# A fused Fourier mixing and GEGLU kernel: the gate of three blocks a batch from two matmuls instead of three, and the channel-128 rows read one slot later

## The chip, the cores and the metric

The kernel runs on one core of a Trainium2 chip. The metric is the device time of one execution in microseconds. TensorE (PE) multiplies, VectorE (DVE), ScalarE (ACT) and GpSimd (POOL) do the elementwise work, and SyncE (SP) issues most DMAs.

## The reference

The input x is 8 batches of 3008 tokens with 256 channels, fp32. The reference takes the real part of a two-dimensional Fourier transform of each batch and puts the result, as 24064 tokens of 256 channels, through a GEGLU block:

```python
X = np.fft.fft(np.fft.fft(x, axis=1), axis=2).real
g = X @ w_gate                       # 256 x 1536
gelu = 0.5 * g * (1.0 + erf(g * inv_sqrt2))
out = (gelu * (X @ w_val)) @ w_out   # 1536 x 256
```

## The kernel before, in words

**Symmetry.** The real part of the transform of a real input repeats itself: the token with index -t and channel -c equals the token t and channel c. The kernel therefore forms only half of the tokens of a batch, in a layout with the channels on the 128 partitions, as an even part E and an odd part O (the two planes of the tile `EO_sb`). The weights are transformed the same way on the chip. The gate of a token is g(E) + g(O), and that of its mirror token is g(E) - g(O) but for one channel, number 128: its row sits in partition 0 of the odd plane although it doesn't change its sign. A third copy of the gate's odd weights, `W["g", "M"]`, is the odd weights times -2, with 0 in that channel. So a gate takes three matmuls into one PSUM bank: E, then O (now the bank holds the token's gate), then M (now it holds the mirror's). The value takes two: E, then O; VectorE makes the mirror's value as 2 (E + correction) - value, where the correction is the channel-128 row (broadcast over the partitions in `EB_sb`) times the weight column `yw`.

**Slots.** Half a batch is 1505 tokens in three chunks of 512, 512 and 481. The 1536 hidden columns are twelve blocks of 128. One (chunk, block) pair is one slot: 36 slots a batch, 288 in all. The function `feed` writes the order of every engine's queue out by hand, slot by slot (the scheduler is off). In a slot stand, in this order:

- `G`: `l1_gate` of this block, matmuls E and O into a bank of `ps_g` (two banks), and the gelu of it on ScalarE (L676)
- `g`: `l1_gate2` of the block before, matmul M and the mirror's gelu (L685)
- `V`: `l1_value` of this block, matmul E into a bank of `ps_v` (three banks), and on VectorE `ve` = EB yw + E (L704)
- four output matmuls (L749) of the chunk before into `ps_o` (one bank)
- POOL's folds of a later batch's input (L216 to L224), where `plan` puts one
- `v`: `l1_value2` of the block before, matmul O, the product h of the token on VectorE (L720), the mirror's value on VectorE (L722), and the mirror's product h on POOL (L724)
- four more output matmuls; after every sixth piece of four, an evacuation of `ps_o` on ScalarE (L769) and four output stores on SyncE's queue (L654)
- the fills, where `plan` puts one: pieces of the Fourier transform of the next batches

All gate, value and mirror matmuls go through one helper, `mm`, and have its line, L660.

**The transform's fills.** For a batch b, `s1t` multiplies folded input by the first factor and evacuates to `S_sb` (L546, L549); `z_write` and `z_read` turn the layout by way of DRAM. Then, for each chunk, `tp_y` computes the channel-128 row and writes it to DRAM (L612, L616, L618), `tp_e` and `tp_o` compute the even and the odd plane of `EO_sb` (L582, evacuated by ScalarE in L592), and `tp_rows` reads the row back twice: into all 128 partitions of `EB_sb` (L626) and into partition 0 of the odd plane of `EO_sb` (L628). The odd planes of the three chunks share a tile, and `tp_o` of a chunk waits for the EO row read of the chunk before. `load_part` loads the input of a later batch: the forward half by SyncE (L152, into `x_raw`) and the mirrored half by an indirect DMA of POOL (L158). `plan` puts these fills at slots: for batches 4 to 7 the nine pieces `tp_y`, `tp_e`, `tp_o` of three chunks lie in slots 18 to 33 of the batch before, for batches 1, 2 and 3 nearer together.

The order within SyncE's queue follows the order of the calls, so that the slot of a fill settles which stores, loads and row writes stand ahead of it.

**Buffers named below.** `gelu` has 5 buffers, `ve` 3, `v` 4, `ps_g` 2, `ps_v` 3, `ps_o` 1 and `ps_dft` (the fills' bank) 2.

Of the kernel before, what the change touches and what calls it, by code (L numbers as in the profile page):

```python
# [9 lines left out]
FP32 = mybir.dt.float32  # L10
BF16 = mybir.dt.bfloat16
AF = mybir.ActivationFunctionType
ALU = mybir.AluOpType
# [15 lines left out]
def kernel(  # L29
# [104 lines left out]
    def v_tile():  # L134
        return work([128, TOK], FP32, "v", 4, "v_sb")

    def osb_tile():
        return work([128, 2, C], FP32, "osb", 3, "out_sb")

    def psum(tag):  # L140
        bufs = {"g": 2, "v": 3, "o": 1, "dft": 2}[tag]
        return psum_pool.tile([128, 512], FP32, tag=tag, bufs=bufs, name=f"ps_{tag}")
# [100 lines left out]
    keep2 = const_pool.tile([128, 1], FP32)  # L243
    dump = const_pool.tile([1, 1], FP32)
    one_h = const_pool.tile([1, 1], BF16)
    yw = const_pool.tile([128, NFC], FP32)
    NGP = NJ * NK
    ff = work([128, 2 * NGP], FP32, "EO", 2, "ff")
    rr = work([128, 2 * NGP], FP32, "EO", 2, "rr")
# [218 lines left out]
    def make_yw(f0, n):  # L468
# [7 lines left out]
            nc.scalar.activation(yw[:, c0 : c0 + nq], ps[:, 0:nq], AF.Copy)  # L476
        return run


    EO_bufs, EB_bufs = {}, {}  # L480
    turn = [0]
# [152 lines left out]
        return tp_e(b, gi, 1, engine)  # L634


    def store(b, gi, sub, sign, osb_half, queue):
        segs = [c for c in cols[gi] if c[0] // 128 == sub]
        m = min(128, chunk_len[gi] - sub * 128)
        for i, (off, k2, w) in enumerate(segs):  # L640
            p0 = off - sub * 128
            lo, hi = (1, w - 1) if sign and k2 == 0 else (0, w)
            if sign:
                t0 = T - k2 - N2 * (hi - 1)
                p1 = m - p0 - hi
            else:
                t0 = k2 + N2 * lo
                p1 = p0 + lo
            dst = ap_replace(
                out,  # L650
                ap=[[N2 * C, hi - lo], [1, C]],
                offset=out.offset + (b * T + t0) * C,
            )
            (nc.sync if i else queue).dma_start(out=dst, in_=_sub(osb_half, [[1, C]], 0, part_start=p1, part_num=hi - lo))  # L654

    def ffn_work(b):
# [5 lines left out]
        def cols_of(ci, fc):  # L662
# [3 lines left out]
                cstate[ci] = {"h": h_tile(), "ps": {}, "pso": {}}  # L666
            return n, c0, E, O, cstate[ci], slice(fc * 128, (fc + 1) * 128)

        def l1_gate(ci, fc):
            def run():  # L670
                n, _, E, O, st, fs = cols_of(ci, fc)
                pg = psum("g")
                mm(pg, n, "g", "E", fs, E, True, False)
                mm(pg, n, "g", "O", fs, O, False, True)
                gl = gelu_tile()
                nc.scalar.activation(gl[:, 0, :n], pg[:, :n], AF.Gelu)  # L676
                st["ps"][fc] = [pg, gl]
            return run

        def l1_gate2(ci, fc):  # L680
            def run():
                n, _, _, O, st, fs = cols_of(ci, fc)
                pg, gl = st["ps"][fc][:2]
                mm(pg, n, "g", "M", fs, O, False, True, skip_group_check=True)
                nc.scalar.activation(_sub(gl, [[-1, n]], TOK + n - 1), pg[:, :n], AF.Gelu)  # L685
            return run
# [88 lines left out]
        for ci in range(NG):  # L775
            nsub = (chunk_len[ci] + 127) // 128
            parts = {k: [f(ci, fc) for fc in range(NFC)] for k, f in (
                ("G", l1_gate), ("V", l1_value), ("g", l1_gate2), ("v", l1_value2))}
            subs = [nsub - 1, *range(nsub - 1)] if last(ci) else range(nsub)
            l2s = [l2_piece(ci, s, g, f) for s in subs for g in range(2) for f in range(0, NFC, L2P)]  # L780
            chunks.append((parts, l2s))
# [91 lines left out]
        make_yw(0, 256)()  # L873
        tp_y(0, 0)()

    NS = NG * NFC

    def plan():

        fill, pool = {}, {}  # L880

        def at(table, s, f):
            table.setdefault(s, []).append(f)

        early = []
        for gi in (1, 2):
            early += [ch(0, 2 * gi), ch(0, 2 * gi + 1, "V"), tp_e(0, gi), tp_o(0, gi, "V"), tp_y(0, gi)]
        for s, f in (
                (0, make_w(0, 256, 256)), (0, make_w(1, 256, 256, engine="V")), (1, make_yw(256, 256)),
                (1, make_w(1, 512, 512, (1,))), (2, make_w(0, 512, 512, (0,), "V")), (2, make_yw(512, 512)),  # L890
                (3, make_w(0, 512, 512, (1,))), (3, make_w(1, 512, 512, (0,), "V")),
                (4, make_w(1, 1024, 512, (1,), "V")), (5, make_w(0, 1024, 512, (0,), "V")), (5, make_yw(1024, 512)),
                (6, make_w(0, 1024, 512, (1,))), (7, make_w(1, 1024, 512, (0,), "V"))):
            at(fill, s, f)
        for i, f in enumerate(early):
            at(fill, (7, 8, 9, 10, 11, 12, 13, 14, 15, 16)[i], f)

        for k, s in ((0, 8), (1, 9), (2, 9)):
            at(fill, s, lambda k=k: load_part(2, k, (load_forward,)))
        for k, s in ((0, 18), (1, 19), (2, 19)):  # L900
            at(fill, s, lambda k=k: load_part(2, k, (load_mirror,)))

        def spread(b, items, s0, s1):

            each = len(items) // NG
            for i, f in enumerate(items):
                s = s0 + i * (s1 - s0) // (len(items) - 1)
                at(fill, s, f)
                if i % each == each - 1:
                    at(fill, s + 1, tp_rows(b, i // each))  # L910

        for b in range(1, B):
            s0 = (b - 1) * NS
            ops = []
            for j0, nj in PIECES:
                ops += fold_ops(b, j0, nj, nc.gpsimd)
            per = len(ops) // 5
            first, n = {2: (s0 - 13, 29), 3: (s0 - 19, 30)}.get(b, (s0 - 22, 32))
            slot_of = [first + i * n // len(ops) for i in range(len(ops))]
            if b == 1:  # L920
                slot_of = [4, 4, 5, 5, 6, 6, 7, 7, 8, 8, 9, 13, 13, 14, 15, 15, 16, 17, 17, 18]
            for s, f in zip(slot_of, ops):
                at(pool, s, f)
            if 1 < b < B - 1:
                for k, piece in ((0, 1), (1, 3), (2, 4)):
                    at(fill, slot_of[piece * per + 1] + 1, lambda b=b, k=k: load_part(b + 1, k))
            s = s0 - 9 if b > 1 else 12
            for i, (jg, piece) in enumerate(((2, 1), (1, 2), (0, 3), (3, 4))):
                ready = slot_of[piece * per + per - 1] + 2
                for g in range(2):  # L930
                    s = max(s + 1, ready)
                    at(fill, s, s1t(b, jg, g))
                if i == 2:
                    at(fill, s + 1, z_write(b, 0, 12))
                if i == 3:
                    at(fill, s + 1, z_write(b, 12, 4))
            at(fill, s + 2, z_read(b))
            items = []
            for gi in range(NG):
                items += [tp_y(b, gi), tp_e(b, gi), tp_o(b, gi)]  # L940
            if b == 1:
                spread(b, items, s + 6, s + 18)
                continue
            assert s + 7 < s0 + NS - 10
            spread(b, items, s + 7, s0 + NS - 3)
        return fill, pool

    def feed():
        blocks, works = [], []
        for b in range(B):  # L950
            for parts, l2s in ffn_work(b):
                works.append(l2s)
                blocks += [(parts, fc) for fc in range(NFC)]
        fill, pool = plan()
        pend, before = [], None

        first = works[0]
        sooner = {8: [first[0]], 9: [first[3]], 10: [first[1]], 11: [first[4]], 13: [first[2]], 14: [first[5]]}
        works[0] = first[6:]
        for i, (parts, fc) in enumerate(blocks):  # L960
            if fc == 0 and i:
                assert not pend
                pend = list(works[i // NFC - 1])
            two = sooner.pop(i, []) if i <= NFC + 2 else [pend.pop(0) for _ in range(2) if pend]
            parts["G"][fc]()
            if i == 0:
                behind_first_gate()
            if before:
                before[0]["g"][before[1]]()
            parts["V"][fc]()  # L970
            if len(two) == 2:
                two.pop(0)()
            for f in pool.pop(i, []):
                f()
            if before:
                before[0]["v"][before[1]]()
            if two:
                two.pop(0)()
            for f in fill.pop(i, []):
                f()  # L980
            before = parts, fc
        assert not fill and not pool
        before[0]["g"][before[1]]()
        before[0]["v"][before[1]]()
        for u in works[-1]:
            u()
# [33 lines left out]
```

## Time and profile before

| what | value |
|---|---|
| median of 3 runs | 630.27 us (629.33 to 630.61) |
| the profiled execution's own time | 629.18 us |
| its span, first to last instruction | 627.0 us |
| granted TensorE clock, mean | 0.996 |
| busy PE / DVE / POOL / ACT | 98% / 92% / 81% / 68% |
| gate and value matmuls | 1440, 0.204 or 0.217 us from start to start |

"Busy" is the share of the span in which an engine has an instruction at work. Matmuls overlap in the records, so their durations (0.37 us at 481 or 512 columns) are longer than the distance between their starts. A wait is written "engine tile line <- who ended it: us in total, times, longest". The timeline gives the start, the duration, the engine, the line, the operation and, in brackets, the idle time before it and what ended it. SPq is SyncE's queue: its rows are the issue of a DMA, not the transfer.

### The profile page before, as it was taken

Reading aid. Unit: us, or ns where it says so; the run is one execution under the profiler, and the core shown is the slowest. Engines: PE = TensorE matmul, PEld = TensorE weight load, DVE = VectorE, ACT = ScalarE, POOL = GpSimd, SP = SyncE. Lnnn points to the kernel's source line nnn. Section 1 sums busy time; section 2 is a strip of 40 time slices with the busy share of each in tenths; the row PEclk is TensorE's granted clock in tenths of the full one; section 3 lists DMA queues with packets and bytes.
Section 4 is the critical chain, followed back from the end, with each engine's and each line's share of the span. In section 5 each row is a group of like instructions: output and inputs, shape, how many; then the busy total and the mean of one; then the engine's idle time right before and its main releaser. Section 6 shows DMA issues by size and latency. Waiting matters only on the chain.

```text
span 627.0 us, 12895 instructions
## 1 busy us (share of the span) xinstructions
PE 612.3 (98%) x4195; PEld 405.1 (65%) x4243; DVE 578.3 (92%) x941; ACT 428.4 (68%) x842; POOL 505.3 (81%) x510
## 2 busy tenths in 40 slices
PE   7999999999999999999999999999999999999997
PEld 3456666666666666666666666666666666666666
DVE  8689989999899999999999998999999999999992
ACT  6777677666776677667676677676676666666661
POOL 8399999989897998879997899969988655555651
PEclk8999999999999999999999999999999999999999
DMA  9961754536353353731645335633212322221123
GB/s 177 227 97 31 210 129 116 144 105 159 99 146 101 98 133 79 184 113 46 160 110 135 101 78 127 148 97 98 62 49 63 91 86 55 51 52 39 42 51 81
DMA packets 54217, 65.40 MB, mean 104 GB/s; under 512 B 7831, under 2 KB 49802, under 8 KB 51754
## 3 DMA queue, kind: packets, MB, share of 16 engines
q1 hardware_dynamic: 47222, 49.03, 30.6%
q0 software_dynamic: 6608, 15.29, 11.4%
q8 instruction: 33, 0.54, 0.4%
q10 hardware_dynamic: 320, 0.26, 0.2%
q14 instruction: 34, 0.28, 0.2%
HBM read 39.65 MB, written 30.17 MB: 111 GB/s over the span
## 4 chain that ended last, share of the span: by engine, by line
PE 93%; ACT 2%; issue 1%; DVE 1%; DMA 1%; POOL 1%; POOLq 0%; ACTq 0%
PE ps_o L749 38%; PE ps_g L660 28%; PE ps_v L660 19%; PE ps_dft L546 2%; PE ps_dft L582 2%; PE ps_o L820 1%; DMA Z_sb<-z 1%; PE ps_dft L443 1%; PE ps_dft L612 0%; ACT gelu_sb L676 0%; POOL h_sb L724 0%; POOL eo_sb L224 0%; DMA out_dram<-out_sb 0%; ACT gelu_sb L685 0%; PE ps_dft L749 0%
## 5 line engine op out<-in xcount | busy, mean ns | idle before, releaser
L724 POOL TENSOR_TENSOR h_sb<-gelu_sb,v_sb 128x512 bf16<-128x512 bf16 (+1 forms) x280 | 319.8, 1146 | 93.1 <-DVE v_sb L722 85.9
L749 PE MATMUL ps_o<-Wo_sb,h_sb 128*128 128x256 bf16 (+1 forms) x2232 | 334.9, 273 | 0.9 <-POOL h_sb L724 0.9
L749 PEld LDWEIGHTS <-h_sb 128*128 128x128 bf16 (+1 forms) x2304 | 228.7, 100 | 112.9 <-POOL h_sb L724 2.6
L676 ACT ACTIVATE gelu_sb<-ps_g 128x512 bf16<-128x512 f32 (+1 forms) x288 | 169.4, 588 | 98.6 <-PE ps_g L660 80.9
L660 PE MATMUL ps_g<-EO_sb,W_sb 128*128 128x512 bf16 (+1 forms) x817 | 228.5, 375 | 3.8 <-ACT gelu_sb L685 0.8
L704 DVE SCALAR_TENSOR_TENSOR ve_sb<-EB_sb,yw,ps_v 128x512 f32<-128x512 bf16 (+1 forms) x280 | 206.3, 737 | 25.9 <-PE ps_v L660 25.0
L660 PE MATMUL ps_v<-EO_sb,W_sb 128*128 128x512 bf16 (+1 forms) x575 | 213.7, 375 | 0.7 <-DVE W_sb L451 0.6
L720 DVE TENSOR_TENSOR h_sb<-gelu_sb,ps_v 128x512 bf16<-128x512 bf16 (+1 forms) x280 | 189.9, 678 | 1.1 <-ACT gelu_sb L685 0.7
L660 PEld LDWEIGHTS <-W_sb 128*128 128x128 bf16 x1440 | 137.2, 98 | 81.1 <-issue 1.8
L722 DVE SCALAR_TENSOR_TENSOR v_sb<-ve_sb,ps_v 128x512 f32<-128x512 f32 (+1 forms) x280 | 187.5, 670 | 0.0
L685 ACT ACTIVATE gelu_sb<-ps_g 128x512 bf16<-128x512 f32 (+1 forms) x288 | 168.7, 586 | 0.0
L769 ACT ACTIVATE out_sb<-ps_o 128x512 f32<-128x512 f32 x92 | 55.0, 598 | 35.7 <-PE ps_o L749 35.6
L224 POOL TENSOR_TENSOR eo_sb<-ab_sb 94x512 bf16<-94x512 f32 (+1 forms) x70 | 77.6, 1111 | 0.5
L549 ACT ACTIVATE S_sb<-ps_dft 96x512 bf16<-96x512 f32 x56 | 32.9, 588 | 14.0 <-PE ps_dft L546 13.9
L592 ACT ACTIVATE EO_sb<-ps_dft 128x512 bf16<-128x512 f32 (+1 forms) x44 | 26.0, 590 | 23.3 <-PE ps_dft L582 22.1
L217 POOL TENSOR_TENSOR ab_sb<-x_raw,x_raw 94x508 f32<-94x508 f32 (+1 forms) x30 | 33.0, 1100 | 0.0
L220 POOL TENSOR_TENSOR ab_sb<-x_raw,x_raw 94x508 f32<-94x508 f32 (+1 forms) x30 | 32.9, 1098 | 0.0
L546 PE MATMUL ps_dft<-eo_sb,G 94*96 94x256 bf16 x119 | 22.5, 274 | 0.2 <-POOL eo_sb L224 0.2
L158 POOL DMA_INDIRECT x_raw<-in_x_dram,idx x18 | 17.1, 948 | 2.9 <-issue 1.1
L582 PE MATMUL ps_dft<-TP,Z_sb 128*128 128x128 bf16 (+1 forms) x184 | 17.8, 218 | 0.0
L582 PEld LDWEIGHTS <-Z_sb 128*128 128x128 bf16 x192 | 14.6, 98 | 1.8 <-DVE Z_sb L534 0.6
L546 PEld LDWEIGHTS <-G 94*96 94x96 bf16 x119 | 13.0, 123 | 1.2 <-issue 0.4
(148 smaller groups left out, 166.2 us busy)
## 6 DMA issues: line engine op xcount, KB each, us to landing
out_dram<-out_sb SPq DMA_DIRECT2D x364, 64.0 KB
x_raw<-in_x_dram SPq DMA_DIRECT2D x10, 768.0 KB
Z_sb<-z SPq DMA_DIRECT2D x7, 768.0 KB
z<-S_sb SPq DMA_DIRECT2D x7, 576.0 KB
EB_sb<-yrow SPq DMA_DIRECT2D x14, 128.0 KB
z<-S_sb SPq DMA_DIRECT2D x7, 192.0 KB
x_raw<-in_x_dram SPq DMA_DIRECT2D x2, 640.0 KB
EB_sb<-yrow SPq DMA_DIRECT2D x7, 120.2 KB
```

The source lines that it names most:

```text
L224: eng.tensor_tensor(_sub(eo, [[C, nj], [1, 128]], j0 * C + g * 128), ab(0, 0, [[1, 128]]), ab(1, 0, [[1, 128]]), op=op)
L546: nc.tensor.matmul(ps[:96, q * C : (q + 1) * C], G[:, j, :], _sub(eo, [[1, C]], j * C), start=(j == js[0]), stop=(j == js[-1]))
L582: nc.tensor.matmul(ps[:, o : o + n], st["Z"][:, pair, g * 128 : g * 128 + 128], _sub(TP, [[1, n]], g * 128), start=True, stop=True)
L660: nc.tensor.matmul(ps[:, :n], W[nm, part][:, fs], src, start=start, stop=stop, **kw)
L676: nc.scalar.activation(gl[:, 0, :n], pg[:, :n], AF.Gelu)
L685: nc.scalar.activation(_sub(gl, [[-1, n]], TOK + n - 1), pg[:, :n], AF.Gelu)
L704: nc.vector.scalar_tensor_tensor(ve[:, :n], EB_bufs[b][:, c0 : c0 + n], yw[:, fc : fc + 1], pv[:, :n], op0=ALU.mult, op1=ALU.add)
L720: nc.vector.tensor_tensor(st["h"][:, fc, 0, :n], gl[:, 0, :n], pv[:, :n], op=ALU.mult)
L722: nc.vector.scalar_tensor_tensor(_sub(vv, [[-1, n]], n - 1), ve[:, :n], 2.0, pv[:, :n], op0=ALU.mult, op1=ALU.subtract)
L724: nc.gpsimd.tensor_tensor(st["h"][:, fc, 1, :n], gl[:, 1, :n], vv[:, :n], op=ALU.mult)
L749: nc.tensor.matmul(pso[:m, half], st["h"][:, fc, sign, h0 : h0 + m], Wo_sb[:, fc, :], start=(fc == 0 and not (first and sign)), stop=(fc = ...
L769: nc.scalar.activation(_sub(osb, [[1, 2 * C]], 0, part_num=m), pso[:m, :], AF.Copy)
```

## The change

In slots 4, 28 and 33 of the batches 1 to 6 (18 blocks in all) the gate takes two matmuls. E goes into the bank alone, and ScalarE copies 2E from it to a new fp32 tile, `e2_sb` (one buffer). A new part `O`, called in `feed` behind the first four output matmuls and ahead of POOL's folds, adds O to the bank, takes the token's gelu on ScalarE, lets VectorE form EB ywg - bank into a buffer of the tag `v`, and lets POOL add `e2_sb` to it: that is the mirror's gate. In the next slot `l1_gate2` takes its gelu from there, and the matmul M is not issued. The column `ywg` is made once, in slot 14 of batch 0. Apart from that, `tp_rows` is called one slot later for every chunk and batch.

```diff
+    def e2_tile():
+        return work([128, TOK], FP32, "e2", 1, "e2_sb")
...
+    def make_ywg():
+
+        fcs = sorted({i % NFC for i in GATE2})
+        ps = psum("dft")
+        for fc in fcs:
+            nc.tensor.matmul(
+                ps[:, fc : fc + 1], W["g", "O"][0:1, fc * 128 : (fc + 1) * 128], one_h, start=True, stop=True)
+        for fc in fcs:
+            nc.scalar.activation(ywg[:, fc : fc + 1], ps[:, fc : fc + 1], AF.Copy, scale=2.0)
...
+    GATE2 = (4, 28, 33)
...
+        def two_gate(ci, fc):
+            return 0 < b < B - 1 and ci * NFC + fc in GATE2
+
         def l1_gate(ci, fc):
             def run():
                 n, _, E, O, st, fs = cols_of(ci, fc)
                 pg = psum("g")
+                if two_gate(ci, fc):
+                    mm(pg, n, "g", "E", fs, E, True, True)
+                    e2 = e2_tile()
+                    nc.scalar.activation(e2[:, :n], pg[:, :n], AF.Copy, scale=2.0)
+                    st["ps"][fc] = [pg, gelu_tile(), e2]
+                    return
                 mm(pg, n, "g", "E", fs, E, True, False)
                 mm(pg, n, "g", "O", fs, O, False, True)
...
+        def l1_gate_odd(ci, fc):
+            def run():
+                if not two_gate(ci, fc):
+                    return
+                n, c0, _, O, st, fs = cols_of(ci, fc)
+                pg, gl, e2 = st["ps"][fc][:3]
+                del st["ps"][fc][2]
+                mm(pg, n, "g", "O", fs, O, False, True, skip_group_check=True)
+                nc.scalar.activation(gl[:, 0, :n], pg[:, :n], AF.Gelu)
+                d = v_tile()
+                nc.vector.scalar_tensor_tensor(
+                    d[:, :n], EB_bufs[b][:, c0 : c0 + n], ywg[:, fc : fc + 1], pg[:, :n],
+                    op0=ALU.mult, op1=ALU.subtract)
+                nc.gpsimd.tensor_tensor(d[:, :n], e2[:, :n], d[:, :n], op=ALU.add)
+                st["ps"][fc][0] = d
+            return run
+
         def l1_gate2(ci, fc):
             def run():
                 n, _, _, O, st, fs = cols_of(ci, fc)
                 pg, gl = st["ps"][fc][:2]
+                if two_gate(ci, fc):
+                    nc.scalar.activation(_sub(gl, [[-1, n]], TOK + n - 1), pg[:, :n], AF.Gelu)
+                    return
                 mm(pg, n, "g", "M", fs, O, False, True, skip_group_check=True)
...
+        at(fill, 14, make_ywg)
...
                 if i % each == each - 1:
-                    at(fill, s + 1, tp_rows(b, i // each))
+                    at(fill, s + 2, tp_rows(b, i // each))
...
             if len(two) == 2:
                 two.pop(0)()
+            parts["O"][fc]()
             for f in pool.pop(i, []):
                 f()
```

More of the change, by code (lines that the diff above doesn't have):

```diff
@@ L245 @@
     one_h = const_pool.tile([1, 1], BF16)
-    yw = const_pool.tile([128, NFC], FP32)
+    yw, ywg = (const_pool.tile([128, NFC], FP32, name=f"yw_{i}") for i in "vg")
     NGP = NJ * NK
@@ L634, in tp_o @@
         return tp_e(b, gi, 1, engine)
+    NS = NG * NFC
+    GATE2 = (4, 28, 33)
     def store(b, gi, sub, sign, osb_half, queue):
@@ L777, in ffn_work @@
             parts = {k: [f(ci, fc) for fc in range(NFC)] for k, f in (
-                ("G", l1_gate), ("V", l1_value), ("g", l1_gate2), ("v", l1_value2))}
+                ("G", l1_gate), ("O", l1_gate_odd), ("V", l1_value), ("g", l1_gate2), ("v", l1_value2))}
             subs = [nsub - 1, *range(nsub - 1)] if last(ci) else range(nsub)
@@ L874, in behind_first_gate @@
         tp_y(0, 0)()
-    NS = NG * NFC
     def plan():
```

## The prediction

> **What bounds the kernel now.** I read the page first (busy shares, chain), then the waits by engine, then the timeline slot by slot. A slot is one block of 128 hidden columns for one chunk; a batch has 36, and "slot 4.28" is batch 4's slot 28. The page:
>
> ```profile
> PE 612.3 (98%) x4195; PEld 405.1 (65%) x4243; DVE 578.3 (92%) x941; ACT 428.4 (68%) x842; POOL 505.3 (81%) x510
> PE 93%; ACT 2%; issue 1%; DVE 1%; DMA 1%; POOL 1%; POOLq 0%; ACTq 0%
> ```
>
> TensorE carries 93% of the chain. A busy matmul row is no proof, so I take the distance between starts. TensorE in slot 4.28:
>
> ```profile
> 378.05 0.78 PE L660 MATMUL ps_g<-EO_sb,W_sb 128*128 128x481 bf16 x3
> 378.66 0.37 PE L660 MATMUL ps_v<-EO_sb,W_sb 128*128 128x481 bf16 x1
> 378.86 0.60 PE L749 MATMUL ps_o<-Wo_sb,h_sb 128*128 128x256 bf16 x4
> 379.30 0.37 PE L660 MATMUL ps_v<-EO_sb,W_sb 128*128 128x481 bf16 x1
> ```
>
> Three gate matmuls in 0.61 us: 0.204 us each at 481 columns (0.217 at 512), and nothing idle. A bare slot of 512 columns takes 1.957 us. So a matmul removed is worth 0.2 us, if nobody makes TensorE wait. Who is close to that? ScalarE in the same place:
>
> ```profile
> 378.25 0.60 ACT L592 ACTIVATE EO_sb<-ps_dft 128x512 bf16<-128x512 f32 x1 [0.62 <-PE ps_dft L582]
> 378.74 0.57 ACT L676 ACTIVATE gelu_sb<-ps_g 128x481 bf16<-128x481 f32 x1
> 379.19 0.58 ACT L685 ACTIVATE gelu_sb<-ps_g 128x481 bf16<-128x481 f32 x1
> ```
>
> It is still evacuating slot 27's fill when slot 28's first matmul starts. The waits hold a DMA that ScalarE waits for, and weight loads that wait for POOL:
>
> ```profile
> PEld L749 <- POOL h_sb L724: 2.6, 6, 1.2
> ...
> ACT EO_sb L592 <- DMA EO_sb<-yrow: 1.1, 2, 0.6
> ```
>
> [...] SyncE's queue around the transform of batch 3,
>
> ```profile
> 225.20 0.53 SPq L626 DMA_DIRECT2D EB_sb<-yrow  x1
> 225.83 0.24 SPq L628 DMA_DIRECT2D EO_sb<-yrow  x1
> 226.22 0.27 SPq L152 DMA_DIRECT2D x_raw<-in_x_dram  x1
> 226.58 0.38 SPq L618 DMA_DIRECT2D yrow<-yrow_sb  x1
> 228.70 3.26 SPq L654 DMA_DIRECT2D out_dram<-out_sb  x4
> 237.14 0.35 SPq L626 DMA_DIRECT2D EB_sb<-yrow  x1
> ```
>
> shows a 1 KB row (L618) issued right behind the 768 KB load x_raw; the next EB read waits for that row until 237.14, 10.5 us. The two reads ahead of the load landed by 230.7 (semaphore events). [...] the trace has 1.25 to 1.27 for an fp32 fold of 508 to 512, and I use 1.15 to 1.2. [...] the like operation here (L704) lasts 0.747 and the next starts 0.65 to 0.72 after it.
>
> **The change, part by part.** 18 blocks (slots 4, 28, 33 of batches 1 to 6).
>
> *Gain.* One matmul less each: 6 x 0.217 + 12 x 0.204 = 3.75 us.
>
> *VectorE* gets 18 differences of about 0.72 us, 13 us. Its three operations of a 512 slot start 1.84 us apart in all when they catch up (0.65 + 0.60 + 0.59) against TensorE's 1.957: 0.11 us to spare in a bare slot, 0.33 with a 0.22 us fill, which follows slots 4 and 28. The delay is gone in three to five slots. Three v banks cover it: in slot 4.4 V starts at 329.43, its bank was free at 327.86, 1.6 us before. I cost it at nothing; without that cover it is up to 13 us.
>
> *The 2E copy* must end before the odd matmul may write the same bank. In slot 4.28 E ends about 378.42, but ScalarE is free only at 378.74: copy to 379.31, odd matmul at 379.36. Its place in the order is after V and four output matmuls, 379.10. TensorE waits 0.26 us. Slot 33 is the same, behind an output evacuation. In slot 4 ScalarE is free and nothing is lost. 12 x 0.26 = **+3.1** (bounds 0 and 6).
>
> *The POOL sum* stands ahead of the second gelu in ScalarE's order, and everything behind that gelu waits. Slot 4.4: h of two blocks before runs to 331.8 on POOL, the sum to 332.95, the gelu starts at 333.02 instead of 332.14. Behind it are the output evacuation (333.5 for a possible 332.9), the next fill and the gelus; ps_o has one bank, so the next output matmuls wait 0.57 us. So in batches 3, 4, 5; in 1 and 6 POOL is ahead, 0.13 each; in batch 2 POOL is late (h of slot 2.2 ends at 185.3), the sum ends near 186.5, the gelu due at 184.1 is 2.4 us late, 2.0 us on TensorE. **+4.0** (1 to 6). In slot 28 the same costs 0.15 three times, **+0.5**.
>
> *POOL at a batch's end.* The sum of slot 33 pushes what follows; there POOL's only rest is 0.52 us:
>
> ```profile
> 394.39 1.10 POOL L724 TENSOR_TENSOR h_sb<-gelu_sb,v_sb 128x481 bf16<-128x481 bf16 x1
> 396.01 1.11 POOL L724 TENSOR_TENSOR h_sb<-gelu_sb,v_sb 128x481 bf16<-128x481 bf16 x1 [0.52 <-DVE v_sb L722]
> 397.26 0.95 POOL L158 DMA_INDIRECT x_raw<-in_x_dram,idx  x1
> 398.23 1.30 POOL L224 TENSOR_TENSOR eo_sb<-ab_sb 94x512 bf16<-94x512 f32 x1
> 399.45 2.24 POOL L724 TENSOR_TENSOR h_sb<-gelu_sb,v_sb 128x481 bf16<-128x481 bf16 x2
> ```
>
> The h at 399.45 is already what a weight load waits 0.21 us for at 400.64. It comes 0.75 us later after batches 2, 3, 4: **+2.25** (0 to 4). Elsewhere there is over 1 us of room. The two yw rows in slot 0.14: **+0.3**.
>
> *The rows.* tp_o of a chunk waits on ScalarE for the EO row read of the chunk before (14 such waits stand in its queue). Moving the issue by one slot moves it past what SyncE has in between. Batch 3 (work done in slots 2.22 to 2.27): the reads now stand behind x_raw instead of ahead of it. So they land with it, 234.4 to 236.9, taken as 236, instead of 230.5; tp_o was ready at 230.55. ScalarE stands 5.5 us, TensorE, two gate banks ahead, all but 0.3 of it, and the 2E copy of slot 2.28 stands behind tp_o and stops TensorE a slot sooner (+0.8): **+6.0** (4 to 7.5). Batch 1 (slots 0.30 to 0.34): the reads move behind four output stores that end issuing at 94.1 and land at 98.9, among the loads; the row lands near 99.3, tp_o was due at 95.33; less 0.4 of slack, **+3.6** (0.9, if it lands 2 us after its issue, to 4.5). Batch 2: behind one more row write, 0.6 us later, and there is no slack now: **+0.5**. Batches 4 and 5: behind four stores too, but tp_o has 8.8 and 8.6 us of slack and some 6 are used, with the mirror load alongside: +0.1 each. Batches 6 and 7: nothing.
>
> *Sum.* Gate: -3.75 + 3.1 + 4.0 + 0.5 + 2.25 + 0.3 = +6.4. Rows: +10.3. Where both stop one slot they are counted twice, -1. That is +15.7 on the profiled execution's 629.2 (span 627.0 and 2.2 around it), 644.9; the median of three runs lies 1.1 above that execution. I say 645.
>
> **Rivals.** (1) *Faster*: the 3.75 us is the whole effect, 626.5. For it: ScalarE is 68% busy, POOL 81%. It needs the row of batch 3 to land before 230.9 though it stands behind 768 KB; that point decides, and the 10.5 us of L618 speaks against it. (2) *The rows are cheap*: most row reads land 1.9 to 2.5 us after issue; [...] 0.9 + 0.5 + 0.3, so 629.2 + 6.4 + 1.7 = 637. (3) *The gate's waits are hidden*, because one stall lets POOL and ScalarE catch up for the next: 629.2 - 3.75 + 10.3 = 636. (4) *VectorE becomes the bound* in the 18 slots: 0.65 x 18 = 11.7 more in place of the POOL and ScalarE waits, and rows 10.3: 629.2 - 3.75 + 11.7 + 10.3 = 647. Against it: 1.6 us of bank lead. (5) The sum of slot 4 does nothing, since the second gelu had room: 641, inside the main case's range.
>
> **Numbers.** Main case 0.55, (2) 0.16, (3) 0.14, (4) 0.07, (1) 0.05, a gain and losses that cancel 0.03. The unknown ends move the main case from 638 to 652; with (2) and (3) in, the range is 634 to 652. A measurement of this kernel tells 0.2% (1.3 us). Faster 0.05, same 0.03, slower 0.92.
>
> **What would show it.** ScalarE waiting 5 us for the DMA of EO_sb once near 231 and 3 to 4 us near 95, TensorE waiting for gelu then; POOL's gelu_sb waits on the sum; TensorE's ps_g waiting for the 2E copy 12 times for about 0.26; weight loads waiting for POOL's h more than 2.6 us in all. No long EO_sb wait makes the row step wrong; VectorE with no idle left and ps_v waiting for it makes the first cover wrong.

## The result, and the profile after

The changed kernel takes **654.7 us** (median of four runs, 652.9 to 655.7) against 630.4 for the kernel before: a ratio of 1.038 (95% interval 1.035 to 1.041). The forecast was 645 with a range of 634 to 652. The side was right, the size too small by 10 us. The profiled execution is 655.3 us, its span 653.5.

The page's line of busy shares, and the chain that ended last:

```profile
PE 621.8 (95%) x4227; PEld 405.1 (62%) x4227; DVE 583.1 (89%) x959; ACT 440.0 (67%) x862; POOL 526.3 (81%) x528
...
PE 12%; DMA 1%; ACT 0%; POOL 0%; DVE 0%; issue 0%; POOLq 0%; SPq 0%; ACTq 0%; DVEq 0%
```

TensorE's share fell from 98% to 95% of a span that is 26.5 us longer: it stands still more. The chain accounts for 13% of the span and is of no use here, so I go to the waits and the timelines. TensorE in slot 4.28, now with two gate matmuls ahead of V and the odd one behind the output matmuls:

```profile
399.20 0.57 PE L677 MATMUL ps_g<-EO_sb,W_sb 128*128 128x481 bf16 x2
399.61 0.37 PE L677 MATMUL ps_v<-EO_sb,W_sb 128*128 128x481 bf16 x1
399.82 0.60 PE L795 MATMUL ps_o<-Wo_sb,h_sb 128*128 128x256 bf16 x4
400.52 0.36 PE L677 MATMUL ps_g<-EO_sb,W_sb 128*128 128x481 bf16 x1
```

A 256-column matmul needs 0.109 us from start to start, so the odd matmul could start at 400.26; it starts at 400.52. That is the predicted 0.26. Why, and what follows, is in ScalarE's, VectorE's and POOL's timelines of the same place:

```profile
399.90 0.57 ACT L696 ACTIVATE e_sb<-ps_g 128x481 f32<-128x481 f32 x1
400.35 0.58 ACT L731 ACTIVATE gelu_sb<-ps_g 128x481 bf16<-128x481 f32 x1
400.98 0.58 ACT L714 ACTIVATE gelu_sb<-ps_g 128x481 bf16<-128x481 f32 x1
...
403.62 0.61 ACT L728 ACTIVATE gelu_sb<-v_sb 128x481 bf16<-128x481 f32 x1 [0.51 <-POOL v_sb L719]
404.14 0.58 ACT L815 ACTIVATE out_sb<-ps_o 128x512 f32<-128x512 f32 x1
```

```profile
401.59 0.72 DVE L716 SCALAR_TENSOR_TENSOR v_sb<-EB_sb,yw_g,ps_g 128x481 f32<-128x481 bf16 x1 [0.85 <-ACT gelu_sb L714]
```

```profile
402.38 1.21 POOL L719 TENSOR_TENSOR v_sb<-e_sb,v_sb 128x481 f32<-128x481 f32 x1 [0.47 <-DVE v_sb L716]
```

The copy ends at 400.47, the odd matmul starts 0.05 later. Then comes a chain that I had not drawn: first gelu, end 401.56; difference, start 401.59, after VectorE stood still for 0.85 us; sum, start 402.38, after POOL stood still for 0.47; second gelu, start 403.62, after ScalarE stood still for 0.51. The output evacuation is behind it. The waits over the whole kernel (us in total, times, longest):

```profile
DVE v_sb L716 <- ACT gelu_sb L714: 16.8, 18, 5.7
POOL v_sb L719 <- DVE v_sb L716: 14.6, 12, 5.4
ACT gelu_sb L728 <- POOL v_sb L719: 14.5, 17, 2.8
...
PE ps_o L795 <- ACT out_sb L815: 5.0, 8, 2.2
PE ps_g L677 <- ACT e_sb L696: 4.9, 1, 4.9
```

All 18 differences wait for the first gelu of the same block, which reads the same PSUM bank, and each starts 0.03 us after that gelu ends: the two take turns, 18 of 18. What makes them take turns, no run shows. I had priced the operation and not this wait.

Of the 18 sums, only 12 wait for the difference. The other six, in slot 4 of batches 2 to 6 and in slot 28 of batch 1, start within 0.02 us of POOL coming free.

The row step shows in ScalarE's waits: two, of 9.1 us in all, predicted as about 5 and 3 to 4. The one wait of TensorE for the 2E copy above, 4.9 us, is its consequence: in slot 2.28 the copy stands behind the waiting tp_o. ScalarE's waits, and SyncE's queue in batch 3:

```profile
ACT EO_sb L605 <- DMA EO_sb<-yrow: 9.1, 2, 5.2
```

```profile
227.79 7.04 SPq L671 DMA_DIRECT2D out_dram<-out_sb  x5
235.25 0.33 SPq L155 DMA_DIRECT2D x_raw<-in_x_dram  x1
235.70 0.36 SPq L639 DMA_DIRECT2D EB_sb<-yrow  x1
236.16 0.23 SPq L641 DMA_DIRECT2D EO_sb<-yrow  x1
```

The reads stand behind the 768 KB load, as forecast: the EO read is issued at 236.16, and ScalarE's wait for it ends at 244.96, 8.8 us later. And POOL, then TensorE, where batch 4 ends:

```profile
413.46 1.21 POOL L719 TENSOR_TENSOR v_sb<-e_sb,v_sb 128x481 f32<-128x481 f32 x1 [0.86 <-DVE v_sb L716]
...
422.82 2.22 POOL L770 TENSOR_TENSOR h_sb<-gelu_sb,v_sb 128x481 bf16<-128x481 bf16 x2
```

```profile
423.98 0.28 PE L795 MATMUL ps_o<-Wo_sb,h_sb 128*128 128x256 bf16 x1 [1.33 <-POOL h_sb L770]
```

POOL loses 1.21 for the sum and 0.86 waiting for the difference; before, it had 0.52 of rest there, and the weight load waited 0.21.

### The profile page after: what moved, and what is told of

Same layout as the page of the kernel before. It is cut to its first block, busy times and chain, and to the rows that moved or that the text cites. A ratio compares the mean times of both kernels' runs of the same rounds, so it can differ in the third digit from the quotient of the medians.

```text
span 653.5 us, 12906 instructions
## 1 busy us (share of the span) xinstructions
PE 621.8 (95%) x4227; PEld 405.1 (62%) x4227; DVE 583.1 (89%) x959; ACT 440.0 (67%) x862; POOL 526.3 (81%) x528
## 5 line engine op out<-in xcount | busy, mean ns | idle before, releaser
L677 PE MATMUL ps_g<-EO_sb,W_sb 128*128 128x512 bf16 (+1 forms) x846 | 231.9, 378 | 11.1 <-ACT gelu_sb L731 5.0
L750 DVE SCALAR_TENSOR_TENSOR ve_sb<-EB_sb,yw_v,ps_v 128x512 f32<-128x512 bf16 (+1 forms) x280 | 206.0, 736 | 28.0 <-PE ps_v L677 27.6
L702 ACT ACTIVATE gelu_sb<-ps_g 128x512 bf16<-128x512 f32 (+1 forms) x270 | 158.9, 588 | 93.0 <-PE ps_g L677 83.4
L731 ACT ACTIVATE gelu_sb<-ps_g 128x512 bf16<-128x512 f32 (+1 forms) x270 | 158.1, 585 | 0.0
L562 ACT ACTIVATE S_sb<-ps_dft 96x512 bf16<-96x512 f32 x56 | 32.8, 586 | 10.3 <-PE ps_dft L559 10.2
L719 POOL TENSOR_TENSOR v_sb<-e_sb,v_sb 128x481 f32<-128x481 f32 (+1 forms) x18 | 22.1, 1226 | 14.6 <-DVE v_sb L716 14.6
L716 DVE SCALAR_TENSOR_TENSOR v_sb<-EB_sb,yw_g,ps_g 128x481 f32<-128x481 bf16 (+1 forms) x18 | 13.1, 728 | 16.8 <-ACT gelu_sb L714 16.8
L728 ACT ACTIVATE gelu_sb<-v_sb 128x481 bf16<-128x481 f32 (+1 forms) x18 | 11.0, 612 | 14.5 <-POOL v_sb L719 14.5
```

Source lines behind the costliest of these rows:

```text
L677: nc.tensor.matmul(ps[:, :n], W[nm, part][:, fs], src, start=start, stop=stop, **kw)
L750: nc.vector.scalar_tensor_tensor(ve[:, :n], EB_bufs[b][:, c0 : c0 + n], yw[:, fc : fc + 1], pv[:, :n], op0=ALU.mult, op1=ALU.add)
```

## The experiments

**Theory.** The row part costs what I said, the gate part 2.5 times as much. The first gelu holds the bank, the difference waits for it, POOL's sum comes after that, and the second gelu, in order on ScalarE, stops what is behind it. **Rivals:** the two parts are worse together than alone; VectorE's extra work is the cost; POOL's time is, and not its place.

### The two parts alone

Rows alone is the kernel before with one number changed; the gate alone is the changed kernel with it put back:

```
-                    at(fill, s + 1, tp_rows(b, i // each))
+                    at(fill, s + 2, tp_rows(b, i // each))
```

> Only the rows' reads move one slot later; every gate block is as before. Theory A (the changed kernel's trace split by place: rows +4.6 at the start of batch 1, about 6.8 in slot 2.29, little in batch 2): 640 to 642, +10 to +11, with ScalarE's EO_sb waits for the DMA near 4 and 5 us. Theory B (the missing 10 us sit in the rows, because the 2E copy behind tp_o is what makes the stall long): without the gate blocks the rows alone cost 5 to 7, near 636.

> The 18 two-pass gate blocks, the rows' reads where they were before. Theory A (the gate step is the one mis-sized, 2.5 to 2.9 us a batch and about 4 in batch 2): 645 to 648, +15 to +17. My prediction's own gate term, +6.4, would give 637. Theory B (the two parts cost more together than alone): 637 to 641, and the two parts' sums fall 5 us or more short of the changed kernel.

Rows: **638.8 us** against 629.5, ratio 1.015 (1.012 to 1.018). Gate: **646.8**, ratio 1.027 (1.024 to 1.030). They cost 9.3 and 17.2 us; the sum of 26.5 is close to the 24.3 of both together, and with intervals of some 2 us on each the 2.2 between them is not clear of noise. The row term (10.3) stands in size. The gate term (6.4) is the one that is wrong.

Stop by stop, from the distances between the starts of consecutive matmuls less what the width of the first needs at full speed (0.217, 0.204, 0.109 us), from 104 us on, put to the releaser that the trace names. This is my sum over the trace, in us:

| TensorE waits for | before | gate alone | difference first | no sum | sum aside |
|---|---|---|---|---|---|
| output evacuation (out_sb) | 0.5 | 8.8 | 6.7 | 1.7 | 1.7 |
| POOL's h | 0.7 | 5.7 | 3.5 | 1.5 | 5.7 |
| second gelu (gate bank) | 1.6 | 4.9 | 3.5 | 1.3 | 1.3 |
| 2E copy | 0 | 3.3 | 2.8 | 2.5 | 3.1 |
| runs at half speed | 0 | 1.5 | 0 | 0 | 0 |

The last three columns are the kernels of the next two sections. Gate alone less before is 21.4 in these rows; less the 3.75 gained that is 17.6, against 17.2 measured.

### The order of the two readers of the bank

```
-                nc.scalar.activation(gl[:, 0, :n], pg[:, :n], AF.Gelu)
                 d = v_tile()
                 nc.vector.scalar_tensor_tensor(d[:, :n], EB_bufs[b][:, c0 : c0 + n], ...)
+                nc.scalar.activation(gl[:, 0, :n], pg[:, :n], AF.Gelu)
```

> As the gate alone, with VectorE's difference put ahead of the first gelu, so it reads the bank first and ScalarE after it. Theory A1 (the difference's wait for the first gelu, 0.6 to 0.85 us a block, is what makes POOL's sum and the second gelu late): sum and second gelu come 0.5 us or more sooner in each block, 5 to 9 us less than the gate alone, 638 to 641. Rival A2 (POOL's 1.2 us sum alone sets the end, and whichever of the two readers goes first the other is late): within 2 us of the gate alone.

**640.2 us**, ratio 1.017 (1.015 to 1.019), 6.6 us less than the gate alone. So the order of the two readers was worth 6.6 of the 17.2. The waits of this kernel:

```profile
ACT gelu_sb L718 <- DVE v_sb L715: 15.4, 18, 1.0
...
POOL v_sb L719 <- DVE v_sb L715: 4.5, 10, 1.1
ACT gelu_sb L728 <- POOL v_sb L719: 4.4, 6, 2.4
```

The last two were 11.2 and 15.7 in the gate alone. Now the first gelu waits for the difference, again 18 of 18: the bank's two readers still take turns. Most of the gain is in slots 28 and 33, where the sum ends 0.5 us sooner. In slot 4 of batches 3 to 5 it ends only 0.05 sooner, since POOL isn't free earlier. And 1.5 of the 6.6, in the profiled executions, are not the order's: batch 2's stop is 2.39 us long in both kernels, but only in the gate alone was it followed by half speed (the last section shows where the two stops lay).

### Without the sum, and with the sum off the way

```
                 nc.vector.scalar_tensor_tensor(
-                    d[:, :n], EB_bufs[b][:, c0 : c0 + n], ywg[:, fc : fc + 1], pg[:, :n],
-                    op0=ALU.mult, op1=ALU.subtract)
-                nc.gpsimd.tensor_tensor(d[:, :n], e2[:, :n], d[:, :n], op=ALU.add)
+                    d[:, :n], e2[:, :n], 1.0, pg[:, :n], op0=ALU.mult, op1=ALU.subtract)
+                nc.gpsimd.tensor_tensor(e2[:, :n], e2[:, :n], d[:, :n], op=ALU.add)   # second kernel only
```

> As the gate alone, without POOL's sum: VectorE forms 2E minus the bank in its one operation, and the second gelu reads that; the correction by the y row is left out for these blocks' mirror half. Theory A2 (POOL's sum on the way to the second gelu, and the 1.2 us that it takes from POOL at a batch's end, carry the loss): 630 to 634, the stalls in slots 3, 5, 29 and 34 all but gone, except the 0.26 of the 2E copy. Theory A1 (the wait on the first gelu carries it): 636 to 641, with half of the stalls left.

> As the kernel without the sum (second gelu straight from VectorE's 2E minus bank, y correction left out), but POOL still does its 1.2 us sum at the same place in its order, into the 2E tile, where nothing reads it. Theory P (POOL's time is what costs: everything behind the sum on POOL comes 1.2 us later, at a batch's end above all): 640 to 646, most of the gate's 17 us are back. Theory C (the sum's place ahead of the second gelu costs): 630 to 634. A split, slot 3 and batch 2 back (7 to 10 us) and slots 5, 29, 34 not: 636 to 640, is what I expect.

Both kernels leave out the channel-128 correction of these blocks' mirror gate. Without the sum: **630.0 us**, ratio 1.0006 (0.9996 to 1.0016). With the sum aside: **636.4**, ratio 1.011 (1.008 to 1.015). Of the 17.2, then, 6.5 are POOL's time and 10.3 the sum's place ahead of the second gelu; 0.4 is the net of everything else, the 3.75 gained included. (The 6.6 of the section above is another cut through the same 17.2, not a third part.) The table agrees: with the sum aside the second gelu stands where it stood in the gate alone, and with its operand ready the evacuation and gelu rows are as without the sum, while POOL's h keeps its 5.7. So in the gate alone the 10.3 are what ScalarE's standing still for the sum costs, the half speed after batch 2's stop included. Without the sum VectorE still does its 18 differences and still waits for the first gelu, and little comes of it:

```profile
DVE v_sb L716 <- ACT gelu_sb L714: 12.6, 18, 1.6
...
PE ps_o L793 <- POOL h_sb L768: 1.0, 4, 0.5
```

Its ve in slot 4.5 comes 0.78 late and then runs 1.85 us apart until it has caught up, in five slots. VectorE's work is hidden, as forecast; what hurts is what hangs on its result. With the sum aside the weight loads wait for POOL's h as they do in the gate alone (6.7 and 7.5 us):

```profile
PEld L794 <- POOL h_sb L769: 6.7, 7, 1.6
```

### The rows and the load

```
-                    at(fill, slot_of[piece * per + 1] + 1, lambda b=b, k=k: load_part(b + 1, k))
+                    at(fill, slot_of[piece * per + 1] + (2 if (b, k) == (4, 0) else 1), lambda b=b, ...)
```

> As the rows alone (638.8), with the 768 KB load of batch 5's forward rows also moved one slot later, so that batch 3's row reads stand ahead of it again. Theory of the order in SyncE's queue: batch 3's 4.7 us go and batch 1's stay, 633.5 to 635. Rival, that a read issued one slot later is late by itself: 638 to 640.

**634.5 us**, ratio 1.007 (1.005 to 1.009): 4.3 less than the rows alone. SyncE's queue in this kernel, and its waits for the row:

```profile
228.41 0.34 SPq L626 DMA_DIRECT2D EB_sb<-yrow  x1
228.86 0.24 SPq L628 DMA_DIRECT2D EO_sb<-yrow  x1
229.20 0.25 SPq L618 DMA_DIRECT2D yrow<-yrow_sb  x1
229.54 0.32 SPq L152 DMA_DIRECT2D x_raw<-in_x_dram  x1
```

```profile
ACT EO_sb L592 <- DMA EO_sb<-yrow: 3.7, 1, 3.7
```

The reads stand in the same slot as in the rows alone, but ahead of the load, and of two waits one is left: batch 1's. So for batch 3 the place behind the load costs, not the slot. For batch 1 that the reads stand behind four output stores is read from the queue alone; it was not taken away.

### Where the second gelu stands

Is there a place where the second gelu finds its sum and stops nobody? Seven kernels move the blocks, the second gelu, or both. The first also puts the difference ahead of the first gelu; the second leaves out the sum, and with it the channel-128 correction.

```
+    GATE_AT = {(1, 10), ..., (6, 10), (6, 16), (6, 23), (6, 29), (6, 35), (7, 7), (7, 14), (7, 22)}
-            return 0 < b < B - 1 and ci * NFC + fc in GATE2
+            return (b, ci * NFC + fc) in GATE_AT
```

> A complete kernel: 13 two-pass gate blocks (difference ahead of the first gelu), all in places where POOL has no fold and ScalarE no evacuation just before: slot 10 of batches 1 to 6, slots 16, 23, 29, 35 of batch 6 and 7, 14, 22 of batch 7; rows' reads as in the kernel before. If POOL's place and the 2E copy are all that cost, the gain is 13 matmuls, 2.7 us, less about 0.3 for the new rows: 626.5 to 628. If VectorE's 0.72 us a block is not caught up, or the longer way to the second gelu still stops TensorE: 630 to 634.

**634.3 us**, ratio 1.007 (1.004 to 1.009): a miss. Although POOL has room there, TensorE stops 0.5 to 1.0 us for each of batch 7's three blocks. The longest, 1.0 in slot 7.15, is not the second gelu's: there the evacuation stands behind the first gelu, which now waits 0.97 us for the difference. In slot 7.8 the second gelu holds up the evacuation behind it, for which TensorE then loses 0.49 us at 566.31:

```profile
565.14 0.63 ACT L728 ACTIVATE gelu_sb<-v_sb 128x512 bf16<-128x512 f32 x1 [0.33 <-POOL v_sb L719]
565.68 0.58 ACT L815 ACTIVATE out_sb<-ps_o 128x512 f32<-128x512 f32 x1
```

> As the kernel without the sum (629.9; y correction left out), with the blocks at slots 4, 13, 20, where ScalarE has just come free. The 2E copy's stall of 0.26 us should go in 12 blocks and the gain is 18 x 0.217: 626 to 627.5. If the 2E copy was no cost, or VectorE's difference is what eats the gain: 629 to 631.

**629.1**, ratio 0.999 (0.998 to 1.000): 0.9 less than without the sum in the old blocks, not the 3 I expected. Slot 20 was a bad choice: slot 19 has an EO evacuation in batches 3 to 6, and in batch 6 TensorE lost 0.25 us for the copy and 0.20 for the evacuation there, as much as two blocks gain. Of the twelve blocks of slots 4 and 13, two lose 0.23 to the copy; at the other ten no stop shows.

```
             if two:
                 two.pop(0)()
+            if before:
+                before[0]["D"][before[1]]()   # second gelu and POOL's h of a two-pass block
```

> As the gate alone (646.8), same blocks, with one change of order: in a two-pass block the second gelu, and POOL's h that reads it, are issued behind the slot's output evacuation in place of ahead of it. Theory C' (what the sum's place costs is that the second gelu stands ahead of an output evacuation, and ps_o has one bank): the stalls of slots 5 and 29 go, 0.65 us twice a batch, and slot 3 and batch 2 stay: 637 to 640. Rival (the gate's PSUM bank, or VectorE held by the first gelu, carries the 10 us): 644 to 647.

**642.9**, ratio 1.021 (1.019 to 1.023), 3.8 less than the gate alone and not the 7 to 10. In the sum over matmul starts the waits for the output evacuation fall to 1.7, as without the sum, but those for the gate bank rise from 4.9 to 8.9. The evacuation alone is not the answer. In ten of the 18 blocks (slots 4 and 28) the second gelu now finds the sum done, 0.15 to 0.4 us before, and follows the evacuation without a wait. Yet TensorE loses 0.2 to 0.7 us behind it: half a microsecond of ScalarE's time now stands ahead of the gelus that free the two gate banks.

> A complete kernel: second gelu behind the evacuation, and 11 blocks in places without folds on POOL or an evacuation ahead of the 2E copy (slot 10 of batches 1 to 6, 16 and 29 of batch 6, 7, 14, 22 of batch 7). If POOL's time, the 2E copy and the evacuation behind the second gelu are all the costs there are, 11 x 0.217 = 2.4 us faster less 0.4 for the y rows: 627 to 628. If it is not below 629, there is a cost that I have not named.

> The second gelu as in the changed kernel (ahead of the evacuation), first gelu ahead of the difference, with 11 blocks only in slots that are 2 more than a multiple of 3: there no evacuation stands right behind the second gelu, nor ahead of the 2E copy (slot 14 of batches 1 to 7, 23 and 35 of batch 6, 5 and 23 of batch 7). Theory C': 627 to 629. Rival, that the way over POOL is too long wherever it stands, as with the 13 blocks before: 632 to 635.

**632.1** (1.005, 1.003 to 1.007) and **632.7** (1.006, 1.004 to 1.008): both miss, for different reasons. With the evacuation ahead (the first), nine of eleven second gelus find the sum done and TensorE still loses 0.2 to 0.7 us for the gate bank behind each. With no evacuation near (the second), all eleven wait for the sum, 11.8 us in all, but TensorE loses less than 0.4 us behind each; more of its loss is at the evacuation and POOL's h (2.6 and 2.0 in the same count, 0.5 and 0.7 before).

```
-            if before:
-                before[0]["D"][before[1]]()
+            if older:                              # the block two slots back
+                older[0]["D"][older[1]]()
...
-            before = parts, fc
+            older, before = before, (parts, fc)
```

> A complete kernel, the last attempt at a gain: the second gelu of a two-pass block and the POOL product behind it are issued one slot later still, behind the output evacuation two slots after the block, so that ScalarE should find POOL's sum done; 10 blocks in places without folds and without the 2E copy's clash (slot 13 of batches 1 to 6, 29 of batch 6, 4, 13, 20 of batch 7). If ScalarE's wait of 1 us for the sum, in order ahead of the next gelus, is the rest of the cost, each block keeps its 0.217 us: 627 to 628. If ScalarE's or VectorE's added work itself is the cost, 630 to 632.

**628.0 us** against 630.2, ratio **0.997** (0.9956 to 0.9984): 10 matmuls are 2.2 us, and 2.2 is the difference of the medians. It is faster than both kernels of the case. Its second gelu among the groups (busy, mean ns, idle ahead of it):

```profile
L718 POOL TENSOR_TENSOR v_sb<-e_sb,v_sb 128x512 f32<-128x512 f32 (+1 forms) x10 | 12.7, 1265 | 5.1 <-DVE v_sb L715 5.0
L715 DVE SCALAR_TENSOR_TENSOR v_sb<-EB_sb,yw_g,ps_g 128x512 f32<-128x512 bf16 (+1 forms) x10 | 7.4, 744 | 3.6 <-ACT gelu_sb L713 3.6
L780 ACT ACTIVATE gelu_sb<-v_sb 128x512 bf16<-128x512 f32 (+1 forms) x10 | 6.3, 629 | 0.0
```

The sum is as long as ever and still waits for the difference; the gelu's own wait is 0.0. But nine of the ten blocks also lie elsewhere than in the 632.1 us kernel. So the same ten places once more, with the second gelu back at one slot after its block:

> The last kernel (628.0) with its 10 blocks where they are, and only the second gelu and POOL's h taken back from two slots after the block to one slot after, still behind the evacuation. If ScalarE's wait for the sum is the cost, 3 to 4 us of it come back: 630.5 to 632.5. If the places were what made the last kernel faster: within 0.7 of 628.

**631.4 us**, ratio 1.0034 (1.0022 to 1.0046): 3.4 of the time come back with that one change (POOL's h moved along, but TensorE's stops for it are 0.9 and 0.7 us in the two kernels). The gelu waits again, in three of the ten blocks,

```profile
L780 ACT ACTIVATE gelu_sb<-v_sb 128x512 bf16<-128x512 f32 (+1 forms) x10 | 6.2, 622 | 2.5 <-POOL v_sb L718 2.5
```

and TensorE's stops for the gate bank rise from 1.6 to 5.4 us. The wait is the smaller part of it. In the seven other blocks the gelu starts 0.5 us after the evacuation in front of it started, with the sum done 0.1 us before, and each loses 0.39 us, more than the 0.217 that it saves: its own half microsecond there delays the gelus behind it. Two slots after the block it stands behind those gelus, in time in which ScalarE would have been idle, and the sum is done 0.3 to 1.3 us before. So its place must satisfy both: the sum done, and room on ScalarE.

## Why the prediction was wrong in size

**Right.** *Gain*: 0.2 us a matmul, and 10 of them bring 2.2 us once nothing waits. *2E copy*: 12 stops were forecast, in slots 28 and 33. In batches 3 to 6 slot 28 loses the 0.26, and slot 4 nothing; batch 2's slot 28 loses 1.8, because there the copy stands behind a tp_o that waits 1.89 for its row. Slot 33 loses the like, 0.24, but not to the copy: with one matmul gone, its output matmuls come 0.2 us sooner and wait for the evacuation ahead of the copy, and the odd matmul behind them finds the copy done. With this 1.2 from the evacuation row the copy's term is 4.5 for a predicted 3.1. *Rows*: 9.3 for 10.3. Batch 3 (slots 2.29, 2.30) was 4.7 for 6.0 and batch 1 (slots 1.0, 1.1) 4.3 for 3.6; batches 2, 4 and 5 nothing, where I had 0.7. The cause was right, the nearness of the sum is partly luck: ScalarE's two waits were 3.7 us each where I had 5.5 and 4.0, TensorE stood still for 3.1 and 2.8, and the rest, about 1.5 each time, is TensorE at half speed afterwards, which the forecast did not have. *VectorE's work*: hidden, shown without the sum.

**Wrong: the POOL sum.** The term was 4.0 + 0.5. In the table the evacuation and gelu rows grow by 11.6, of which 1.2 is slot 33's, and half speed adds 1.5: **11.9 in place of 4.5**. Stop by stop that is about 3.7 in slot 28 for 0.5, 7.6 in slot 4 for 4.0, and 0.4 behind slot 33 for nothing.

- Slot 28: given 0.15 three times, it costs about 0.64 in each of batches 2 to 6. This is the step that failed: I let the sum start when POOL's queue was free, drew that line for slot 4 alone, and only put a number to slot 28. There (in five of six batches) POOL is free, and the sum waits for the difference (0.47 us in slot 4.28), which waits until the first gelu has ended (0.85). This chain was not in the forecast.
- Slot 4: "Slot 4.4: h of two blocks before runs to 331.8 on POOL, the sum to 332.95, the gelu starts at 333.02 instead of 332.14." In batches 2 to 6 the sum does start when POOL comes free. But in batches 3 to 6 POOL comes free later and the sum takes 1.27 in place of the 1.15 that I had estimated, so that the gelu starts 3.9 us after the slot's first value matmul and not 3.6. TensorE loses 0.72 more than before where I had 0.57, and the same in batches 1 and 6, where I had POOL ahead and 0.13.
- Batch 2's late gelu alone is 2.4 us of standing still and the 1.5 of half speed, for a predicted 2.0.

**Wrong: POOL at a batch's end**, 2.25. POOL's h grew by 5.0. I took 0.75 an end, 1.2 of sum less 0.52 of rest, and left out that POOL, in order, also waits 0.86 for the difference: the ends of batches 2, 3 and 4 lose 1.4 each. Those of 1 and 5, where I saw a microsecond of room, lose 0.4 each.

**The rivals.** (1) Faster: fell, on the rows and on the gate. (2) The rows are cheap: fell, 9.3. (3) The gate's waits are hidden: fell, 17.2. (4) VectorE becomes the bound, 647: nearest in number, and wrong: without the sum VectorE does the same work and the time is that of before. (5) The sum of slot 4 does nothing: fell; in batch 4 TensorE stops 0.49 and 0.36 behind it, where before it stopped 0.13.

## What to carry to other kernels

Before pricing an operation that is "hidden", write down what it waits for, its bank's other readers included, and which in-order engine waits for its result (here 16.8 us of VectorE's standing still for the bank's other reader, and 14.5 of ScalarE's for POOL's sums); the operation's engine may have room while its consumer has none. When a new chain crosses three engines, look for a place of its last step where the result is done and the engine has idle time ahead of the next thing that somebody waits for, and not where the old step stood: the same ten passes lost 1.7 us with it one slot after the block and gained 2.2 with it two slots after. Small reads that somebody waits for go ahead of large loads in their queue: here that was worth 4.3 us.

## What the hardware showed that I had not expected

After a stop TensorE ran at half speed. Windows of the rows alone, batch 3 (busy times, then granted clock, DMA share, GB/s):

```profile
238.00:240.00 2.00, 0.00 (x0) 0.00 (x0) 0.00 (x0) 1.45 (x4) 0.82 (x1) 1.00 0.39 117
240.00:242.00 2.00, 1.88 (x6) 0.85 (x6) 0.13 (x1) 1.43 (x4) 1.11 (x1) 0.55 0.00 0
242.00:244.00 2.00, 2.00 (x11) 1.06 (x9) 1.39 (x3) 0.27 (x2) 0.00 (x0) 0.59 0.00 0
244.00:246.00 2.00, 2.00 (x16) 1.38 (x16) 1.21 (x3) 2.00 (x5) 1.44 (x2) 1.00 0.13 31
```

TensorE stood still for 2.9 us (3.1 counted from the starts), and then 481 columns took 0.40 us in place of 0.204 for some 3 us, which made the stop 1.5 us dearer.

In the changed kernel the granted clock falls to 0.50 at 99.55, 195.13 and 246.33 us and returns to 1.00 3.413 us later each time; the distances between the falls are 28 and 15 times 3.413 us, so the falls lie on one grid. I cut all fifteen profiled executions, from 60 us to the last matmul, into windows of 3.413 us on this grid and summed in each the time in which TensorE stood still. The clock fell at the end of all seven windows with 2.06 us or more, and of none with 1.93 or less. In the changed kernel the three windows before the falls have 2.71, 2.23 and 3.17 us, and no other has over 1.76. What sets the grid and the limit, no run shows.

So the length of a stop does not decide alone. Batch 2's stop of 2.4 us in the gate alone lies with 2.0 us in one window, which has 2.1 in all, and the clock fell. The same stop with the difference first lies with 1.1 and 1.3 us in two windows, and it did not; nor did it after a stop of 2.7 us in the rows with the load behind, split into 1.0 and 1.8. In these runs a stop of about 2 us or more cost 1.5 us more than itself or did not, depending on where it lay on the grid.
